# Attention products in one run per head pair, single-pass turns of copied softmax weights, and q stored as high, low, high

## The chip, the core and the metric

The kernel runs on one core of one Trainium2 chip. Five engines work side by side: TensorE (PE in the profile; its weight loads PEld), VectorE (DVE), ScalarE (ACT), GpSimd (POOL) and SyncE (SP), which issues every DMA here. The metric is the device time of one launch in microseconds (us); lower is better. Times shown are medians of several runs.

## What is computed

Attention with a top-k mask on 2 batches, 8 heads, 576 tokens and head size 64, then two dense blocks over all 1152 tokens of width 512:

```
scores = scale * q @ k.T                      # per batch and head, 576 x 576
kth    = the 32nd largest of each row
attn   = softmax(where(scores >= kth, scores, -1e9))
x      = (attn @ v), heads side by side       # 1152 x 512
p      = domain_probs / sum(domain_probs)     # 1152 x 4
x      = sum over 4 experts e of p[:, e] * (relu(x @ w1[e]) @ w2[e])   # 512 -> 1024 -> 512
out    = ((x @ w_a) * (x @ w_b)) @ w_out      # 512 -> 1536 -> 512, weights in double precision
```

## The kernel before

**Tiles and groups.** Tokens are taken in nine tiles of 128: four per batch, and a mixed one (MIX) with the last 64 tokens of both batches. `SIZES` puts them in groups of 1, 2, 3 and 3. A step is one tile and one pair of heads; there are 36, in the order group, head pair, tile. n is the number of the step: 0 to 3 belong to group 0, 4 to 11 to group 1, 12 to 23 to group 2, 24 to 35 to group 3, the last one of each pair being the mixed tile.

**One step.** `scores` multiplies q and k, both split into a high and a low part in fp32r. k's parts lie one above the other on the partitions (k high, k low), turned by TensorE. q is stored with four blocks of 64 per tile, high, high, low, low, and two turned operands come of them: (high, high) and (low, low). ACT moves the scores to SBUF. `masked` finds the 32 largest of each row on VectorE (four MAX8, three MATCH_REPLACE8 per head), then makes the masked exponentials: ACT, GpSimd, ACT, a sum, a reciprocal, and ACT's scaling in place (L773). At step `URGENT` = 3 `hurried` takes a shorter way over VectorE. `weigh` turns the scaled weights (`e`) on TensorE, four blocks of 128 columns and one of 64 per head (L821, L822), evicts them with two ACT instructions per head (L828, L832), and multiplies by v: for each tile one run of ten pairs of f32 matmuls (twenty for the mixed tile), the two heads of a pair side by side in the array's columns (L848). The last block of v (`vrem`) has 64 real rows and 64 of zeros. When a head pair of a group is done, ACT and VectorE split the sum into `xs` (L866, L868).

**The experts.** When all four head pairs of a group are there, its tokens go through the four experts: `plain` for group 0 in f32, `experts` for the others in fp32r with split operands (three matmuls for one). Weights come by DMA into four slots (`raw`), are split by ACT (L889) and GpSimd or VectorE (L890). `gated` at the end does the last block for all tokens.

**What sets the order.** All work is recorded as operations with a key, a cost and what they wait for; `Plan` simulates the engines with these costs and emits each engine's instructions in the order so found, the best of 42 tries. Instructions then execute in that fixed order on each engine. On TensorE keys put attention first, experts' matmuls (1000 and up) fill. The plan's price of a DMA is on L88: 500 ns to issue, 320 GB/s, 2100 ns to land; of a turn on L320; of a run with v on L854. `mm` (L458) and `tr` (L461) issue every matmul and every turn, so the profile knows them by those two lines, and by the names of what they read: a turn reads `identr`; turns of `low` are softmax weights (f32), of `big` q and k (fp32r), of `ys` the experts' sums. A run with v reads `low` with `128*64`; score matmuls read `big` with 288 columns.

**Memory.** SBUF is laid out in regions (`big`, `mid`, `raw`, `low`) with numbered slots; a region is used again by a later stage when the earlier slots are done. `krem`, the split last rows of k, has a fixed place at the start of `big`.

## Time and profile before

| | |
|---|---|
| time, median of 3 runs | 841.81 us (841.73 to 843.05) |
| span of the profiled execution | 838.8 us, from its first to its last instruction |
| TensorE busy | 816.7 us, 97% |
| VectorE busy | 702.5 us, 84% |
| ACT busy | 540.0 us, 64% |
| GpSimd busy | 265.7 us, 32% |
| DMA queue of SyncE | 116 MB, 43.9% of 16 engines' span |

The page gives no time of the profiled execution but its span; the median of the timed runs is 3.0 us longer, which stands for what lies around the span. Matmuls are pipelined: the duration of one in the profile is longer than its place in the stream, so costs on TensorE are read from start to start. An f32 matmul leaves two records, an fp32r matmul and any turn one.

### The profile page before, as it was taken

To read this page: it belongs to the slowest core of one execution; us is meant where nothing else is said; L and a number is where in the kernel's file an instruction comes from. 1 tells how busy PE (TensorE), PEld (TensorE's weight loads), DVE (VectorE), ACT (ScalarE), POOL (GpSimd) and SP (SyncE) were. 2 spreads that over 40 slices of the span, in tenths; PEclk is the share of its full clock that TensorE was granted. 3 is DMA by queue.
4 is the path that set the end of the run, shared out by engine and by line. 5 is a ranking of instruction groups with operands and counts; after the bars stand their busy time and mean duration, and the time that the engine had idled before them with its cause. 6 is when DMAs were issued, how large, how long until landed. Compare 5 with 4: busy or idle time off the path is not lost.

```text
span 838.8 us, 14118 instructions
## 1 busy us (share of the span) xinstructions
PE 816.7 (97%) x5177; PEld 730.4 (87%) x5177; DVE 702.5 (84%) x1363; ACT 540.0 (64%) x1037; POOL 265.7 (32%) x250
## 2 busy tenths in 40 slices
PE   7599999999999999999999999999999999999997
PEld 6477877789898999899989998999898989999996
DVE  7999999999999999999969998545235888899723
ACT  6888887989999989887666556343125535344220
POOL 3634443797998966763110000000000000000000
PEclk9999999999999999999999999999999999999999
DMA  5849977754555435233335656433002322323003
GB/s 176 286 120 313 308 240 236 218 175 165 192 172 178 148 138 182 84 95 101 101 126 169 208 158 220 126 125 101 1 1 63 89 78 73 101 78 100 26 1 113
DMA packets 83509, 117.06 MB, mean 140 GB/s; under 512 B 10608, under 2 KB 54640, under 8 KB 83440
## 3 DMA queue, kind: packets, MB, share of 16 engines
q1 hardware_dynamic: 83440, 116.17, 43.9%
q8 instruction: 40, 0.66, 0.3%
q14 instruction: 29, 0.24, 0.1%
HBM read 109.07 MB, written 7.08 MB: 138 GB/s over the span
## 4 chain that ended last, share of the span: by engine, by line
PE 80%; DVE 14%; ACT 4%; issue 1%; POOL 0%; DVEq 0%; POOLq 0%; ACTq 0%
PE ps L458 76%; DVE low L723 7%; DVE low L731 6%; PE ps L461 5%; ACT mid L889 1%; ACT low L773 1%; ACT low L762 1%; ACT low L703 0%; ACT low L828 0%; ACT low L754 0%; ACT big L514 0%; ACT big L655 0%; DVE low L794 0%; POOL low L758 0%; DVE low L1175 0%
## 5 line engine op out<-in xcount | busy, mean ns | idle before, releaser
L723 DVE MAX8 low<-low 128x8 f32<-128x576 f32 x288 | 203.3, 745 | 2.8 <-ACT low L703 2.6
L458 PE MATMUL ps<-xs,mid 128*128 128x384 f32 (+1 forms) x1152 | 204.6, 320 | 0.3 <-DVE mid L963 0.2
L458 PE MATMUL ps<-mid 128*128 128x512 f32 x768 | 196.8, 394 | 0.0
L458 PEld LDWEIGHTS ps<-xs,mid 128*128 128x128 f32 x1152 | 184.9, 188 | 9.1 <-DVE xs L1024 0.5
L458 PEld LDWEIGHTS ps<-mid 128*128 128x128 f32 x768 | 140.0, 188 | 22.6
L731 DVE MATCH_REPLACE8 low<-low 128x576 f32<-128x576 f32 x216 | 159.1, 741 | 0.0
L458 PE MATMUL ps<-xs,big 128*128 128x384 f32 x864 | 152.6, 335 | 0.0
L458 PEld LDWEIGHTS ps<-xs,big 128*128 128x128 f32 x864 | 150.2, 188 | 1.5 <-DVE xs L1024 0.3
L889 ACT ACTIVATE mid<-raw 128x1024 fp32r<-128x1024 f32 x96 | 101.7, 1062 | 44.4 <-PE ps L458 33.9
L890 POOL TENSOR_TENSOR mid<-raw,mid 128x1024 fp32r<-128x1024 f32 x48 | 115.2, 2407 | 13.8 <-ACT mid L889 9.5
L758 POOL TENSOR_TENSOR low<-low 128x576 f32<-128x576 f32 x70 | 99.6, 1438 | 31.9 <-ACT low L754 30.4
L890 DVE TENSOR_TENSOR mid<-raw,mid 128x1024 fp32r<-128x1024 f32 x48 | 59.3, 1236 | 24.6 <-ACT mid L889 24.1
L959 ACT ACTIVATE mid<-ps 128x384 fp32r<-128x384 f32 (+1 forms) x96 | 43.8, 457 | 52.5 <-PE ps L458 51.5
L458 PE MATMUL ps<-big,mid 128*128 128x512 f32 x324 | 76.1, 391 | 0.0
L458 PEld LDWEIGHTS ps<-big,mid 128*128 128x128 f32 x324 | 60.5, 188 | 12.6 <-DVE low L1175 0.6
L963 DVE SCALAR_TENSOR_TENSOR mid<-ps,mid 128x384 fp32r<-128x384 f32 (+1 forms) x96 | 48.3, 505 | 25.0 <-ACT mid L959 24.6
L1154 ACT ACTIVATE low<-ps 128x384 f32<-128x384 f32 x36 | 17.7, 492 | 69.7 <-PE ps L458 69.3
L773 ACT ACTIVATE low<-low 128x576 f32<-128x576 f32 x70 | 51.3, 774 | 12.1 <-DVE low L770 12.0
L762 ACT ACTIVATE low<-low 128x576 f32<-128x576 f32 x70 | 54.4, 778 | 2.2 <-POOL low L758 2.1
L461 PE MATMUL ps<-identr,low 128*128 128x128 f32 (+1 forms) x360 | 50.6, 283 | 4.7 <-ACT low L773 4.0
L754 ACT ACTIVATE low<-low 128x576 f32<-128x576 f32 x70 | 52.3, 776 | 4.3 <-POOL low L748 4.3
L703 ACT ACTIVATE low<-ps 128x576 f32<-128x576 f32 x72 | 46.6, 650 | 11.4 <-POOL low L758 7.5
(90 smaller groups left out, 1024.8 us busy)
## 6 DMA issues: line engine op xcount, KB each, us to landing
raw<-in_moe_w_dram SPq DMA_DIRECT2D x122, 512.0 KB, 3.8
big<-kscr SPq DMA_DIRECT2D x20, 576.0 KB, 5.5
low<-in_v_dram SPq DMA_DIRECT2D x24, 256.0 KB, 3.9
low<-in_moe_w_a_dram SPq DMA_DIRECT2D x12, 512.0 KB, 4.3
low<-in_moe_w_b_dram SPq DMA_DIRECT2D x12, 512.0 KB, 3.8
low<-in_moe_w_out_dram SPq DMA_DIRECT2D x12, 512.0 KB, 3.6
kscr<-big SPq DMA_DIRECT2D x8, 576.0 KB, 4.7
ys<-in_moe_w_dram SPq DMA_DIRECT2D x6, 512.0 KB, 5.2
```

Source lines behind the costliest of these rows:

```text
L458: nc.tensor.matmul(out, l, r, **kw)
L461: nc.tensor.transpose(out, a, i)
L703: S, lambda: nc.scalar.activation(s.ap.rearrange("p (c n) -> p c n", c=2), at.ap[:, :, 0:HALF], AF.Copy),
L723: 62 + 1.04 * width, lambda at=at, cs=cs: nc.vector.max(m8v()[:, x, cs], at()), key + 0.02 * r, [done],
L731: lambda at=at, cs=cs: nc.vector.match_replace(out=src[1](), in_to_replace=m8v()[:, x, cs], in_values=at(), imm_value=LOW),
L754: S, lambda x=x, s=s: nc.scalar.activation(e[x].ap, s.ap, AF.Relu, bias=endv()[:, x, 1:2], scale=-STEEP),
L758: pool_(S), lambda x=x, s=s: nc.gpsimd.tensor_tensor(e[x].ap, s.ap, e[x].ap, op=ALU.subtract), ks, [a], [s, e[x]]
L762: lambda x=x: nc.scalar.activation(e[x].ap, e[x].ap, AF.Exp, bias=endv()[:, x, 0:1], scale=scale, accum_out=sums.ap[:, x:x + 1]),
L773: S, lambda x=x: nc.scalar.activation(e[x].ap, e[x].ap, AF.Copy, scale=sums.ap[:, x:x + 1]),
L889: hi = scalar(1024, lambda: nc.scalar.activation(u.ap[:, 0:1024], r.ap, AF.Copy), 500 + s, [ld], [u, r], sbuf=True)
L890: sub = lambda eng: eng.tensor_tensor(u.ap[:, 1024:2048], r.ap, u.ap[:, 0:1024], op=ALU.subtract)
L963: lambda h=h, p=p: nc.vector.scalar_tensor_tensor(h.ap[:, n:2 * n], p.ap[:, 0:n], 0.0, h.ap[:, 0:n], op0=ALU.max, op1=ALU.subtract),
```

## The change

- `weigh` keeps the turned weights of all tiles of a group and head pair, and multiplies them by v in one run at the last tile. A tile's weights for both heads lie in one buffer of 2 x 576 columns. Nine blocks of 128 are turned in place of ten: the fifth holds the last 64 columns of head 0 and the first 64 of head 1. k of the odd head has its last rows first, and `vrem` has its zeros in the other half for odd heads. Evictions are one per head, 512 and 640 columns wide.
- From step 8 (`MOVED`) each head's scaled weights are copied by a DMA from `e` to a buffer `er` of type fp32r, and the turns read that one.
- q is stored as high, low, high; the two turned operands are the overlapping views (high, low) and (low, high). The subtraction that makes the low part writes 64 columns per tile and head in place of 128.
- `krem` becomes slots of `big`, where `er` follows it. `e` has three slots of two heads in place of six of one, `pt` four of 1152 in place of three of 640. The scratch area for DMAs issued by GpSimd is set to 1024 bytes per partition.
- The plan's price of a run with v is 1092 ns a tile and 350 ns a run (1245 a tile before); of fp32r turns 46 + 85 for each of all but two + 64.

```diff
+AV, SWITCH = 1092, 350
+MOVED = 8
-    krem = [big.t[0:REM, b * 1024:(b + 1) * 1024].rearrange("p (h a d) -> p h a d", a=2, d=D) for b in range(B)]
-    big.at = 2048
+    krems = big.slots("krem", B, 1024)
...
+    ers = big.slots("er", 2, 2 * S)
+    ers.rank = 0.5
-    es = low.slots("e", 6, S)
-    pts = low.slots("pt", 3, (M4 + 1) * 128)
+    es = low.slots("e", 3, 2 * S)
+    pts = low.slots("pt", 4, 2 * S)
...
+    def split2(dst, src, m, key, after, tiles, eng):
+        a = scalar(
+            m * 2 * D, lambda: nc.scalar.activation(dst()[:, :, ::2], src().unsqueeze(2).to_broadcast([128, m, 2, D]), AF.Copy),
+            key, after, tiles, sbuf=True,
+        )
+        sub = lambda e: e.tensor_tensor(dst()[:, :, 1], src(), dst()[:, :, 0], op=ALU.subtract)
...
-                        tr(p[:, i, lh], sqv()[:, j, i, lh].rearrange("p a d -> p (a d)"), identr)
+                        tr(p[:, i, lh], sqv()[:, j, i, lh:lh + 2].rearrange("p a d -> p (a d)"), identr)
...
 def weigh(pair, i, ed, n):
+        (e, done), p, ptd = ed, pts.tile(n), []
+        f, idt = e, ident
+        if n >= MOVED:
+            f, idt = ers.tile(n), identr
+            done = [load(
+                lambda j=j: f.ap[:, j * S:(j + 1) * S].bitcast(F32), lambda j=j: e.ap[:, j * S:(j + 1) * S], n + 0.1, [done[j]], [e, f], S * 512,
+            ) for j in range(2)]
...
+        for j in range(2):
+            at = atts.tile(kt)
+            def turn(j=j, at=at):
+                a = (at.ap if f is e else at.ap.bitcast(F32R)).rearrange("p b n -> p (b n)")
+                if j:
+                    tr(a[:, MAIN - 128:MAIN], f.ap[:, MAIN:MAIN + 128], idt)
                 for m in range(M4):
-                    tr(a[:, m], e.ap[:, m * 128:(m + 1) * 128], ident)
-                tr(a[0:REM, M4], e.ap[:, MAIN:S], ident)
+                    c0 = j * (S + REM) + m * 128
+                    tr(a[:, j * MAIN + m * 128:j * MAIN + (m + 1) * 128], f.ap[:, c0:c0 + 128], idt)
-            o = tensor(4 * TURN_F + 80, turn, kt, [done, ready], [at, e])
+            hold = (M4 + j) * TURN_F if f is e else 46 + (M4 + j - 2) * 85 + 64
+            o = tensor(hold, turn, kt, [done[j], done[0], ready], [at, f])
...
+        pair.turned.append((t, p, ptd))
+        if i < T - 1:
+            return
         def emit():
+            for i, (t, p, _) in enumerate(pair.turned):
+                for r0, r1, b in [(0, 128, t[0])] if t != MIX else [(b * REM, (b + 1) * REM, b) for b in range(B)]:
                     for m in range(M4 + 1):
                         for j in range(2):
...
-        pair.od.append(tensor(
-            1245, emit, n + 0.6, ...
+        pair.od = [tensor(
+            T * AV + SWITCH, emit, n + 0.6, ...
```

On TensorE, the second tile of group 2's first head pair, before: its ten turns (`identr,low`, in two lots of four and one), and its run with v (`low`, `64x128`, and `vrem`), among score matmuls (`big`, `128x288`) and experts' matmuls of group 1 (`xs,mid` and `mid`):

```order
L461 MATMUL ps<-identr,low 128x128 x4
L461 MATMUL ps<-identr,low 64x128
L458 MATMUL ps<-xs,mid 128x256 x3
L461 MATMUL ps<-identr,low 128x128 x4
L461 MATMUL ps<-identr,low 64x128
L458 MATMUL ps<-mid 128x512 x9
L458 MATMUL ps<-low 64x128 x8
L458 MATMUL ps<-low,vrem_73 64x128 x2
L458 MATMUL ps<-big 128x288 x8
L458 MATMUL ps<-mid 128x512 x12
```

The first and the third tile of that pair have such a run of their own. In the changed program the same engine at the end of that pair:

```order
L464 MATMUL ps<-identr,big 128x128 x4
L461 MATMUL ps<-xs,mid 128x256 x18
L464 MATMUL ps<-identr,big 128x128 x5
L461 MATMUL ps<-big 128x288 x4
L461 MATMUL ps<-xs,mid 128x256 x6
L461 MATMUL ps<-low 64x128 x8
L461 MATMUL ps<-low,vrem_72 64x128 x2
L461 MATMUL ps<-low 64x128 x8
L461 MATMUL ps<-low,vrem_73 64x128 x2
L461 MATMUL ps<-low 64x128 x8
L461 MATMUL ps<-low,vrem_73 64x128 x2
L461 MATMUL ps<-big 128x288 x4
```

The three tiles' products stand in one run, and the turns, four and five, read `big`. In the whole program runs with v go from 36 to 16, f32 turns of softmax weights from 360 to 72, and 252 fp32r turns are new.

On TensorE, the end of group 1 in the changed program: group 0's experts (`raw,low`, `xf,ys`) run out, the last tile's nine turns, one more of those matmuls, the first three of group 1's experts, and the product of two tiles:

```order
L461 MATMUL ps<-xf,ys 128x128 x8
L461 MATMUL ps<-raw,low 128x512 x3
L464 MATMUL ps<-identr,big 128x128 x9
L461 MATMUL ps<-raw,low 128x512
L461 MATMUL ps<-xs,mid 128x256 x3
L461 MATMUL ps<-big 128x288 x4
L461 MATMUL ps<-low 64x128 x8
L461 MATMUL ps<-low,vrem_72 64x128 x2
L461 MATMUL ps<-low 64x128 x8
L461 MATMUL ps<-low,vrem_72 64x128 x2
```

Before, four matmuls of `raw,low` stood behind the last product of group 1, and none of group 1's experts ahead of it.

On SyncE's queue, the changed program in group 2: copies of softmax weights (`big<-low`) stand among loads of experts' weights (`raw<-in_moe_w_dram`), of v and of stored k (`big<-kscr`):

```order
L443 DMA raw<-in_moe_w_dram 128x4x256 x2
L443 DMA low<-in_v_dram 128x2x256
L443 DMA big<-kscr 128x1152
L443 DMA raw<-in_moe_w_dram 128x2x512
L443 DMA big<-low 128x576 x2
L443 DMA low<-in_q_dram 128x2x64
L443 DMA low<-in_q_dram 128x2x128
L443 DMA big<-low 128x576
L443 DMA raw<-in_moe_w_dram 128x2x512
L443 DMA big<-low 128x576
L443 DMA big<-kscr 128x1152
L443 DMA raw<-in_moe_w_dram 128x4x256 x2
```

The `big<-low` rows, 56 in the whole program, are new; a load behind one is issued after it.

## Rows read from the trace of the kernel before

**Rows 1.** The page's first line: span and instructions.

```profile
span 838.8 us, 14118 instructions
```

**Rows 2.** Stretches: us, busy of PE, PEld, DVE, ACT, POOL, clock, DMA, GB/s.

```profile
0.00:75.00 75.00, 58.41 (x390) 47.87 (x391) 69.76 (x156) 57.88 (x125) 33.58 (x54) 0.98 0.70 216
75.00:153.00 78.00, 77.90 (x582) 60.58 (x581) 78.00 (x169) 67.16 (x138) 33.06 (x39) 1.00 0.79 257
153.00:165.00 12.00, 11.62 (x96) 10.26 (x95) 12.00 (x27) 12.00 (x24) 10.78 (x9) 1.00 0.79 246
165.00:435.00 270.00, 269.58 (x2007) 243.09 (x2006) 261.91 (x541) 235.77 (x471) 188.25 (x151) 1.00 0.45 142
435.00:834.00 399.00, 398.99 (x2112) 368.64 (x2110) 279.86 (x472) 167.16 (x283) 0.00 (x0) 1.00 0.31 97
```

**Rows 3.** Chain that ended last: start, us, what (two pieces).

```profile
141.10 1.33 DVE low L723 x2
...
164.80 17.92 PE ps L458 x118
```

**Rows 4.** Timeline, TensorE, end of group 1: start, us, line, what.

```profile
142.12 1.28 PE L461 MATMUL ps<-identr,low 128*128 128x128 f32 x10
143.23 1.06 PE L458 MATMUL ps<-xf,ys 128*128 128x128 f32 x8
...
145.73 1.09 PE L458 MATMUL ps<-low 128*64 128x128 f32 x16
...
153.14 1.64 PE L458 MATMUL ps<-xs,mid 128*128 128x256 f32 x9
```

**Rows 5.** Timeline, TensorE, a mixed tile's run and q's turns.

```profile
323.73 0.69 PE L458 MATMUL ps<-low 128*64 128x64 f32 x16
324.25 0.29 PE L458 MATMUL ps<-low,vrem 128*64 128x64 f32 x4
324.36 0.64 PE L458 MATMUL ps<-low 128*64 128x64 f32 x16
324.83 0.29 PE L458 MATMUL ps<-low,vrem 128*64 128x64 f32 x4
...
326.22 0.64 PE L461 MATMUL ps<-identr,big 128*128 128x128 f32 x6
326.69 1.81 PE L458 MATMUL ps<-xs,mid 128*128 128x384 f32 x9
328.34 0.62 PE L461 MATMUL ps<-identr,big 128*128 128x128 f32 x6
```

**Rows 6.** Timeline, TensorE, 36 matmuls of 384 columns and what follows.

```profile
441.75 6.41 PE L458 MATMUL ps<-xs,mid 128*128 128x384 f32 x36
447.99 0.86 PE L458 MATMUL ps<-mid 128*128 128x512 f32 x3
```

**Rows 7.** Timeline, TensorE, one tile's run with v and its neighbours.

```profile
204.81 0.70 PE L458 MATMUL ps<-big 128*128 128x288 f32 x4
205.35 0.51 PE L458 MATMUL ps<-xs,mid 128*128 128x256 f32 x3
205.79 1.10 PE L458 MATMUL ps<-low 128*64 128x128 f32 x16
206.71 0.39 PE L458 MATMUL ps<-low,vrem 128*64 128x128 f32 x4
...
207.66 1.59 PE L458 MATMUL ps<-xs,mid 128*128 128x256 f32 x12
```

**Rows 8.** DMA issues: names, queue, count, KB each, median us to landing.

```profile
low<-in_v_dram SPq DMA_DIRECT2D x24, 256.0 KB, 3.9
...
kscr<-big SPq DMA_DIRECT2D x8, 576.0 KB, 4.7
...
out_dram<-low SPq DMA_DIRECT2D x8, 256.0 KB, 2.0
```

**Rows 9.** Waits of SyncE's queue: line, releaser, us in total, times, longest.

```profile
SPq L440 <- DVE mid L890: 150.6, 40, 9.1
```

More of the change, by code (lines that the diff above doesn't have):

```diff
@@ L396, in body @@
     wraws = raw.slots("wraw", 4, 1024)
[L397 removed]
+    low = Region("low", 12300 + 4 * 1152 - 3 * 640, F32)
     kraws = low.slots("kraw", 2, 2 * M4 * D)
@@ L519, in split @@
         return [a, b]
+    def split2(dst, src, m, key, after, tiles, eng):
[4 more added lines that the diff above has]
+        sub = lambda e: e.tensor_tensor(dst()[:, :, 1], src(), dst()[:, :, 0], op=ALU.subtract)
+        if eng == "DVE":
+            b = vector(dve(m * D) + 30, lambda: sub(nc.vector), key, [a], tiles, port=True)
+        else:
+            b = gpsimd(pool_(m * D), lambda: sub(nc.gpsimd), key, [a], tiles)
+        return [a, b]
     krem_done, vrem_done, qrem_done, kept = {}, {}, [], {}
+    krem = [krems.tile(b) for b in range(B)]
+    kremv = lambda b: krem[b].ap[0:REM].rearrange("p (h a d) -> p h a d", a=2, d=D)
     def keys(b, h2, key, eng):
@@ L670, in start_pair @@
             if b not in vrem_done:
-                vrem_done[b] = load(lambda b=b: vrem[b][0:REM], lambda b=b: last_rows(v, b), n - 2.4, (), (), 131072, since=14e3)
+                vrem_done[b] = [
+                    load(lambda b=b, j=j: vrem[b][j * REM:(j + 1) * REM, j::2], lambda b=b, j=j: last_rows(v, b)[:, j::2], n - 2.4, (), (), 65536, since=14e3)
+                    for j in range(2)
+                ]
         return pair
@@ L713, in masked @@
         urgent = n == URGENT
-        e = [es.tile(n) for _ in range(2)]
+        ep = es.tile(n)
+        ev = lambda x: ep.ap[:, x * S:(x + 1) * S]
         last, firsts = [], []
@@ L740, in masked @@
             key = n + (0.4 if urgent else 0.001) * x
-            last.append(top(x, [lambda s=s: s.ap, lambda x=x: e[x].ap], 0, TOPK // 8, S, key, sd[x][1]))
+            last.append(top(x, [lambda s=s: s.ap, lambda x=x: ev(x)], 0, TOPK // 8, S, key, sd[x][1]))
         if urgent:
@@ L838, in weigh @@
-        groups = [(0, 128, t[0])] if t != MIX else [(b * REM, (b + 1) * REM, b) for b in range(B)]
-        bs = [b for _, _, b in groups]
-        def emit():
-            for r0, r1, b in groups:
-                for m in range(M4 + 1):
-                    for j in range(2):
-                        vt = pair.v[b].ap.rearrange("p (h m d) -> p h m d", h=2, m=M4)
-                        l = vt[:, j, m] if m < M4 else vrem[b][:, pair.h + j]
-                        mm(
-                            ov()[j * D:(j + 1) * D, i, r0:r1], l, pt[j].ap[:, m * 128 + r0:m * 128 + r1],
-                            start=(m == 0), stop=(m == M4),
-                        )
@@ L853, in weigh @@
-        pair.od.append(tensor(
-            1245, emit, n + 0.6, [zeroed] + ptd + sum((pair.vd[b] for b in bs), []) + [vrem_done[b] for b in bs], [pair.o] + pt + [pair.v[b] for b in bs]
-        ))
+        (e, done), p, ptd = ed, pts.tile(n), []
[5 more added lines that the diff above has]
+            ) for j in range(2)]
@@ new lines, in weigh @@
+        pair.turned.append((t, p, ptd))
+        if i < T - 1:
+            return
+        def emit():
+            for i, (t, p, _) in enumerate(pair.turned):
+                for r0, r1, b in [(0, 128, t[0])] if t != MIX else [(b * REM, (b + 1) * REM, b) for b in range(B)]:
+                    vt = pair.v[b].ap.rearrange("p (h m d) -> p h m d", h=2, m=M4)
+                    for m in range(M4 + 1):
+                        for j in range(2):
+                            l = vt[:, j, m] if m < M4 else vrem[b][:, pair.h + j]
+                            c0 = j * (S + REM) + m * 128 if m < M4 else MAIN
+                            mm(ov()[j * D:(j + 1) * D, i, r0:r1], l, p.ap[:, c0 + r0:c0 + r1], start=(m == 0), stop=(m == M4))
@@ L856, in weigh @@
+        bs = batches(pair.tiles)
+        pair.od = [tensor(
+            T * AV + SWITCH, emit, n + 0.6, [zeroed] + sum((d for _, _, d in pair.turned), []) + sum((pair.vd[b] + vrem_done[b] for b in bs), []),
+            [pair.o] + [p for _, p, _ in pair.turned] + [pair.v[b] for b in bs],
+        )]
         if i == T - 1:
```

102 lines of the change are left out of this document (46 added, 56 removed).

## The prediction

> **What bounds the kernel now.** I read the stretches first, then the chain of work, then single runs of TensorE. The profiled execution spans 838.8 us [rows 1]; the median of the timed runs is 841.8, so 3.0 us lie around the span, and I carry them unchanged. In the stretches [rows 2] the reader is to see TensorE fill up: 58.4 us of the first 75, then 77.90 of 78, 11.62 of 12, 269.58 of 270 and 398.99 of 399, always at a granted clock of 1.00. Busy alone proves little where matmuls are pipelined, but the idle time does: 0.42 us in the 270. The chain [rows 3] says the same in another way: until 141.1 it is made of VectorE's top-k pieces (MAX8, MATCH_REPLACE8), then of a few ACT pieces, and from 164.8 on of TensorE runs. So there are two regimes. Up to about 153 us VectorE and TensorE are both full (78.00 and 77.90 of 78): VectorE with the top-k of groups 0 and 1, TensorE with group 0's experts as filling. From 153 on TensorE alone sets the time, and an instruction taken from it there is worth what it held. VectorE isn't far behind: 261.9 of 270 us between 165 and 435.
>
> **The change part by part.** *Turns.* A tile's softmax weights were ten f32 turns; such a run starts at 142.12, and the next kind of matmul at 143.23 [rows 4]: 1.11 us, 0.111 each. Now it is nine. For the eight tiles before step 8 that is 8 x 0.11 = 0.9 us, all before 153. For the other 28 the nine are fp32r turns. The trace has those for q: a run of six starts at 326.22, nine 384-column matmuls at 326.69, and the next run at 328.34 [rows 5]. A 384-column matmul takes 0.173 us ((447.99 - 441.75) / 36, [rows 6]), so the six took 2.12 - 1.56 = 0.56 us, 0.093 each, entry and exit included. Nine are 0.84; a tile saves 1.11 - 0.84 = 0.27 us. The 24 tiles of groups 2 and 3 lie behind 153: 24 x 0.27 = 6.5 us. The four of group 1 give 1.1 before it.
>
> By the Trainium skill, "TensorE: Matmul & The Clock Gate", section "LDWEIGHTS (loading the stationary operand)", a 128-column load takes columns / 1.2, 107 ns, and no kind of data is excepted. The f32 turn agrees with that, the fp32r turn at 93 ns doesn't; what the rule would leave of the change is a rival below.
>
> *Runs with v.* Before, each of the 36 tiles has its own run. One of them: four score matmuls at 204.81, three 256-column ones at 205.35, the run at 205.79, four score matmuls, and the next kind at 207.66 [rows 7]. From 205.35 to 207.66 are 2.31 us; less four score matmuls at 0.135 ((205.35 - 204.81) / 4) and three of 0.115 (two thirds of 0.173) this leaves 1.42 for the run. How much of it is entering and leaving? Its first sixteen records (an f32 matmul leaves two, and the two heads run as a pair, so eight pairs) take 0.92; the mixed tile shows two such groups in one run, 0.52 for the first and 0.47 for the second [rows 5], so 0.05 of the 0.92 is entry. 0.87 / 8 = 0.109 a pair, ten pairs 1.09: 0.33 us of a run are the switch. The order has 16 runs in place of 36. Groups 2 and 3 lose 16 switches behind 153, 5.3 us; group 1 loses 4 before it, 1.3.
>
> *The sum on TensorE*: 6.5 + 5.3 = 11.8 us behind 153, 0.9 + 1.1 + 1.3 = 3.3 before it.
>
> *What of the 3.3 counts.* There VectorE's pace stays as it is; TensorE can gain only as far as group 1's last product doesn't wait for it. Step 11's turns are at 142.12, its product at 145.73, group 1's experts start at 153.14 [rows 4]. In the new order only one matmul of filling is left between the last turns and that product, and the path to it gets a copy and both tiles' products. Bounds: nothing, and all of 3.3; I take the middle, 1.6, since neither end has a nearer row.
>
> *The copies* are the wait that the change adds. From step 8 each head's weights (288 KB, 56 copies) go through SyncE's queue from one place of SBUF to another before TensorE turns them. No row shows such a copy. 256 KB land in 2.0 us towards HBM and in 3.9 from it, 576 KB in 4.7 [rows 8]; the plan counts (line 88) 500 ns, 294,912 bytes at 320 GB/s and 2100 ns, 3.5 us. So a copy can be 1.5 us earlier or 1.2 us later than planned. TensorE executes in a fixed order: behind a late turn wait the experts' matmuls. If each of 24 tiles waits 1.2, that is 28.8 us; if TensorE, once it has slipped by 1.2, stays behind ACT and VectorE, which don't wait for it, it is 1.2 once. I take 1.5, near the second end: waits for ACT's scaling, planned in the same way, left only 0.42 us idle in 270 [rows 2]. By the Trainium skill, "SBUF — State Buffer", section "The DMA setup-cost knee", a transfer takes 2 us plus its bytes at 436 GB/s: an estimate of 2.7 us here, no wait, and a forecast of 828.4. The rows have 3.9 for 256 KB, where it gives 2.6, so I don't go by it.
>
> Behind a copy on SyncE's queue stand weight loads. SyncE spends 150.6 us waiting until VectorE frees a slot, up to 9.1 at once [rows 9]: loads go out when a slot of four falls free, so some microseconds more are hidden by the three others. If this cover went, each tile would cost TensorE what the copy waited: the rival on the slow side.
>
> *At nothing:* half the evictions of turned weights (72 for 144, one of each pair wider) and half-size subtractions for q, because ACT (235.8 of 270) and GpSimd (188.3) don't hold up a TensorE that is idle for 0.42; the zeroing, the smaller scratch area and the tiles' new places, because no instruction on the path waits for them. q's turns stay as many.
>
> *Sum:* 11.8 + 1.6 - 1.5 = 11.9 us; a span of 838.8 - 11.9 = 826.9, and with the 3.0 around it **829.9 us**.
>
> **The rivals.** *Late copies or late attention, partly.* The turns wait 0.3 us in each of the 24 tiles, 7.2 us, or the attention ends late: in the new order only 24 matmuls of 384 and 36 of 512 columns of group 2's experts stand behind the last product (before: 96 and 84), 24 x 0.173 + 36 x 0.23 (four thirds of it) = 12.4 us of cover. For it: VectorE's 261.9 of 270. Against it: if VectorE can't go faster at all, it is late by the 11.8 that TensorE gains, still inside the 12.4. The time: 841.8 - 13.4 + 7.2 = 835.6.
>
> *The turns gain only the tenth.* Were an fp32r turn bound as an f32 one, a tile would save 0.11: 24 x 0.11 = 2.6 in place of 6.5, 0.4 in place of 1.1 before: 834.2. Against it: 0.093 for 0.111 in the trace. By the Trainium skill, "TensorE: Matmul & The Clock Gate", section "LDWEIGHTS (loading the stationary operand)", it would be so.
>
> *SyncE's order makes it slower.* A copy at the head of the queue waits for ACT, and with it the loads behind. From 11.8 / 24 = 0.5 us of TensorE's waiting per tile the gain is gone; at 0.8, two thirds of the 1.2 above, it is 841.8 - 13.4 + 19.2 = 847.6. For it: all loads share this one queue and SyncE already waits most of the time. Against: four slots of lead.
>
> *The change doesn't do what it says*: excluded for the number of runs and the kinds of turn, which the order shows; whether a turn of copied data is as quick as one of q's is in the second rival.
>
> **How the numbers follow.** The forecast 0.68, alone with a range of 825.5 (15.1 saved, and 1.2 more if each switch is 0.06 dearer than read) to 834 (copies that cost 4 in place of 1.5, and nothing of the 3.3); partly late 0.17; tenth turn alone 0.05; slower 0.10. Within 0.2% (1.7 us) a measurement of this kernel can't tell a change. Faster by more: 0.68 + 0.05 + 0.13 of the partly late = 0.86; same: 0.04 of that and 0.01 of the slow one; slower 0.09. The range that leaves out the slow rival and a few hundredths on each side is 825.5 to 839.
>
> **What would show it.** Runs with v: 16, each costing TensorE about 0.33 + T x 1.09 us. fp32r turns of four and five: about 0.37 and 0.47 us from start to start of what follows, less that work's own time. TensorE's idle time between 165 and the end of the attention: under 2 us, with DMA as its releaser where the copies are late. The first experts' matmul of group 1 between 150 and 154 us. The last run with v at about 440 us, and no gap at the start of group 3's experts. Copies landing in 2.0 to 4.7 us. I am wrong if the runs cost more than counted (a run of 20 or 30 matmuls slower per pair than 0.109), if the idle time in 165 to 435 grows beyond 5 us, or if the start of group 1's experts moves past 156.

## The result and the profile after

The changed kernel took 846.93 us (median of 4 runs, 845.69 to 848.14) against 841.77 before: a ratio of 1.0067, 95% interval 1.0055 to 1.0079. 829.9 us were forecast, with 839 as the upper end. The profiled span is 843.9 us, 5.1 more than [rows 1].

First the stretches of the changed kernel, as in [rows 2], and two short ones behind them (us; busy time of PE, PEld, DVE, ACT, POOL; clock; DMA share; GB/s):

```profile
0.00:75.00 75.00, 55.41 (x365) 45.27 (x366) 68.10 (x152) 56.95 (x115) 30.90 (x53) 0.89 0.66 204
75.00:153.00 78.00, 73.84 (x569) 58.00 (x569) 77.48 (x168) 63.32 (x115) 32.39 (x38) 1.00 0.92 301
153.00:165.00 12.00, 11.53 (x90) 10.14 (x85) 12.00 (x29) 11.61 (x25) 7.75 (x10) 1.00 0.66 233
165.00:435.00 270.00, 260.93 (x1954) 237.59 (x1954) 257.86 (x531) 230.30 (x420) 182.29 (x147) 0.98 0.58 188
435.00:834.00 399.00, 398.99 (x2152) 369.19 (x2151) 285.78 (x483) 174.05 (x293) 3.24 (x4) 1.00 0.32 99
275.00:300.00 25.00, 18.00 (x102) 15.66 (x100) 23.27 (x49) 21.17 (x40) 16.07 (x16) 0.90 0.51 177
300.00:325.00 25.00, 24.11 (x173) 21.91 (x173) 23.43 (x51) 21.56 (x44) 11.99 (x15) 0.89 0.40 129
```

The same two short stretches of the kernel before:

```profile
275.00:300.00 25.00, 25.00 (x197) 22.94 (x197) 24.95 (x55) 23.78 (x53) 20.50 (x17) 1.00 0.58 194
300.00:325.00 25.00, 25.00 (x203) 22.34 (x199) 24.78 (x54) 22.71 (x47) 17.32 (x15) 1.00 0.29 96
```

TensorE, never idle there before, is idle for 7 of 25 us, and its clock falls. I added up every idle gap between TensorE's instructions in both traces. Before: 17.5 us in all, 17.1 of them ahead of 165. After: 33.3 us, of which 19.6 ahead of 75 (16.6 before), 4.6 in 75 to 165 (0.5 before) and 9.1 between 165 and the last run with v of group 2 (0.4 before). The rest of the span, "not idle" below, fell from 821.3 to 810.6 us. So 10.7 us less of work and 15.8 more of idling make the 5.1.

What TensorE does in 288 to 306 of the changed kernel (timeline: start, us, line, what, and in brackets the idle time ahead with its releaser):

```profile
288.10 0.66 PE L464 MATMUL ps<-identr,ys 128*128 128x128 f32 x4 [1.50 <-DVE xs L1051]
290.74 0.80 PE L461 MATMUL ps<-xs,mid 128*128 128x384 f32 x3 [1.99 <-DVE xs L1051]
...
294.38 1.57 PE L461 MATMUL ps<-big 128*128 128x288 f32 x8
299.34 0.72 PE L464 MATMUL ps<-identr,big 128*128 128x128 f32 x4 [3.39 <-DMA big<-low]
300.96 0.85 PE L464 MATMUL ps<-identr,big 128*128 128x128 f32 x5 [0.89 <-DMA big<-low]
...
303.86 1.83 PE L461 MATMUL ps<-low 128*64 128x128 f32 x16
```

And the same place before, 14 us earlier:

```profile
289.67 1.09 PE L458 MATMUL ps<-low 128*64 128x128 f32 x16
...
292.55 0.93 PE L458 MATMUL ps<-mid 128*128 128x512 f32 x3
293.32 0.62 PE L461 MATMUL ps<-identr,big 128*128 128x128 f32 x6
293.78 2.49 PE L458 MATMUL ps<-xs,mid 128*128 128x384 f32 x13
```

The run at 303.86 is that of step 23, the last of group 2, whose experts can't be finished without it. I call its start the product. Before, it stood at 289.67, and group 1's experts, the filling, lasted until 293.1: the two met almost exactly, and group 2's experts followed without a gap. After, the filling is used up at 282.2 (eleven microseconds earlier: TensorE has less to do, and the new order puts more of the filling ahead of the attention) and the run comes at 303.86, fourteen later. Between the two TensorE has the tip of group 2's experts, the turns and the scores, and waits. The clock pays too:

```profile
290.00:295.00 5.00, 4.26 (x21) 4.13 (x22) 5.00 (x14) 2.89 (x6) 2.23 (x4) 0.67 0.55 206
295.00:300.00 5.00, 1.61 (x11) 1.28 (x9) 4.56 (x9) 3.84 (x6) 1.41 (x2) 0.84 0.31 118
300.00:305.00 5.00, 4.11 (x26) 3.77 (x27) 5.00 (x13) 3.78 (x8) 1.78 (x3) 0.50 0.02 5
```

At 300 to 305, behind the idle 3.39 us, the granted clock is 0.50: 1.2 in place of 2.4 GHz. Busy time times the share of clock that is missing, from 290 to 305, is 3.7 us (0.33 x 4.26 + 0.16 x 1.61 + 0.50 x 4.11). I had counted 15.1 us less of work (11.8 + 3.3); 10.7 were seen. These 3.7 are of the size of the difference, but the sum isn't closed: the first 75 us ran at a lower clock too, 0.89 in place of 0.98 [rows 2].

The waits of TensorE in the changed kernel (us in total, times, longest), the four largest:

```profile
PE ps L464 <- ACT low L793: 8.3, 3, 4.2
PE ps L464 <- DMA big<-low: 7.2, 6, 3.4
PE ps L464 <- ACT low L722: 3.8, 3, 2.9
PE ps L464 <- POOL big L520: 2.7, 1, 2.7
```

L793 is ACT's scaling of the softmax weights, L722 its move of the scores to SBUF, L520 GpSimd's subtraction in the splits. These three lie ahead of 75 us, but for 0.4 of L722's; of the waits on copies 2.4 us lie between 75 and 165 and 4.8 behind 165.

Copies and the loads of weights (rows as in [rows 8]):

```profile
raw<-in_moe_w_dram SPq DMA_DIRECT2D x122, 512.0 KB, 4.4
big<-low SPq DMA_DIRECT2D x56, 288.0 KB, 3.7
```

The copies landed in 2.3 to 6.4 us. What TensorE executes was sized right. Two copied heads' turns and a run with v over three tiles:

```profile
227.49 0.46 PE L464 MATMUL ps<-identr,big 128*128 128x128 f32 x4
227.78 0.59 PE L461 MATMUL ps<-xs,mid 128*128 128x256 f32 x3
...
228.91 0.54 PE L464 MATMUL ps<-identr,big 128*128 128x128 f32 x5
229.28 0.77 PE L461 MATMUL ps<-big 128*128 128x288 f32 x4
229.88 0.87 PE L461 MATMUL ps<-xs,mid 128*128 128x256 f32 x6
230.69 1.09 PE L461 MATMUL ps<-low 128*64 128x128 f32 x16
...
231.83 1.04 PE L461 MATMUL ps<-low 128*64 128x128 f32 x16
...
232.92 1.04 PE L461 MATMUL ps<-low 128*64 128x128 f32 x16
...
234.11 0.81 PE L461 MATMUL ps<-big 128*128 128x288 f32 x4
```

Four turns and five take 0.29 and 0.37 us from start to start, 0.073 each, where q's six took 0.47 in the same reading [rows 5], 0.078 each. A tile inside a run costs 1.09 us (232.92 - 231.83), as forecast, and the whole run 3.54 (234.11 - 229.88, less six 256-column matmuls at 0.115), where 0.33 + 3 x 1.09 = 3.60 were forecast.

### The profile page after: what moved, and what is told of

Same layout as the page of the kernel before. It is cut to its first block, busy times and chain, and to the rows that moved or that the text cites. A ratio compares the mean times of both kernels' runs of the same rounds, so it can differ in the third digit from the quotient of the medians.

```text
span 843.9 us, 14148 instructions
## 1 busy us (share of the span) xinstructions
PE 806.0 (96%) x5141; PEld 724.2 (86%) x5141; DVE 704.7 (83%) x1363; ACT 536.2 (64%) x965; POOL 256.6 (30%) x249
## 4 chain that ended last, share of the span: by engine, by line
PE 86%; ACT 4%; DMA 4%; DVE 3%; POOL 1%; issue 1%; SPq 0%; POOLq 0%; ACTq 0%; DVEq 0%
PE ps L461 81%; PE ps L464 6%; DMA big<-low 3%; DVE low L743 1%; DVE low L751 1%; ACT low L793 1%; ACT low L722 1%; DMA raw<-in_moe_w_dram 1%; POOL mid L917 1%; ACT big L671 0%; ACT low L774 0%; POOL big L520 0%; SPq L443 0%; DVE xs L1051 0%; ACT low L859 0%
## 5 line engine op out<-in xcount | busy, mean ns | idle before, releaser
L461 PE MATMUL ps<-xs,mid 128*128 128x384 f32 (+1 forms) x1152 | 207.2, 322 | 2.7 <-DVE xs L1051 2.0
L461 PE MATMUL ps<-mid 128*128 128x512 f32 x768 | 194.3, 393 | 0.1
L461 PEld LDWEIGHTS ps<-xs,mid 128*128 128x128 f32 x1152 | 184.2, 189 | 10.9 <-DVE xs L1051 2.5
L464 PEld LDWEIGHTS ps<-identr,big 128*128 128x128 f32 (+1 forms) x476 | 53.0, 146 | 27.7 <-ACT low L722 5.2
L464 PE MATMUL ps<-identr,big 128*128 128x128 f32 (+1 forms) x476 | 61.4, 260 | 15.3 <-DMA big<-low 7.2
L986 ACT ACTIVATE mid<-ps 128x384 fp32r<-128x384 f32 (+1 forms) x96 | 44.3, 463 | 38.2 <-PE ps L461 37.7
L990 DVE SCALAR_TENSOR_TENSOR mid<-ps,mid 128x384 fp32r<-128x384 f32 (+1 forms) x96 | 48.2, 505 | 22.8 <-ACT mid L986 22.2
L793 ACT ACTIVATE low<-low 128x576 f32<-128x576 f32 x70 | 51.9, 785 | 7.1 <-DVE low L790 7.0
## 6 DMA issues: line engine op xcount, KB each, us to landing
big<-low SPq DMA_DIRECT2D x56, 288.0 KB, 3.7
```

The costliest lines, as they stand in the source:

```text
L461: nc.tensor.matmul(out, l, r, **kw)
L464: nc.tensor.transpose(out, a, i)
L793: S, lambda x=x: nc.scalar.activation(ev(x), ev(x), AF.Copy, scale=sums.ap[:, x:x + 1]),
L986: n, lambda h=h, p=p: nc.scalar.activation(h.ap[:, 0:n], p.ap[:, 0:n], AF.Relu), -1000, [o], [h, p]
L990: lambda h=h, p=p: nc.vector.scalar_tensor_tensor(h.ap[:, n:2 * n], p.ap[:, 0:n], 0.0, h.ap[:, 0:n], op0=ALU.max, op1=ALU.subtract),
```

## The experiments

Five theories are tested. A: before group 2's last product TensorE doesn't set the time, so what it saves there turns into idling, and the copies' latency adds to it. B: the order that the planner drew was unlucky (it draws lateness at random and keeps its best order). C: the start is late by 1.9 us. D: a turn that waits for its copy holds PSUM slots which the scores of three steps later need, and so holds up VectorE. E: the time that TensorE saves goes to the filling too early, which takes ACT, VectorE and GpSimd from the attention.

All runs are in one table. "Step 23" is the end of that step's last MAX8 (the 192nd of the trace), "product" the start of group 2's last run with v, "filling" the start of the last matmul of group 1's experts, "idle" TensorE's before 165 and from there to 5 us past that run; "not idle" the span less all idling. The time is a median, and each ratio is to the kernel before as measured beside that kernel (medians of 840.72 to 841.37; 841.77 for the changed one). The columns behind the ratio come from one profiled execution, which lies up to 1.7 us from the median (843.66 for 845.35 in per_tile_runs). Where an expectation counts matmuls of the filling ahead of a step's scores, it counts the steps from one: its step 24 is n = 23.

| kernel | us | ratio to before, 95% | step 23 | product | filling | idle | not idle |
|---|---|---|---|---|---|---|---|
| before | 841.77 | | 271.6 | 289.7 | 293.1 | 17.1, 0.4 | 821.3 |
| before_other_draws | 842.83 | 1.0008-1.0026 | 272.7 | 289.3 | 297.1 | 16.7, 0.6 | 824.0 |
| before_third | 842.23 | 1.0002-1.0019 | 271.5 | 287.6 | 297.6 | 18.4, 1.0 | 822.0 |
| q_split_only | 841.79 | 0.9998-1.0017 | 271.3 | 284.9 | 296.4 | 19.1, 0.0 | 821.7 |
| fill_early | 841.34 | 0.9996-1.0013 | 277.4 | 292.6 | 289.1 | 18.0, 0.4 | 820.7 |
| after | 846.93 | 1.0055-1.0079 | 284.0 | 303.9 | 282.2 | 24.2, 9.1 | 810.6 |
| other_draws | 842.04 | 0.9992-1.0013 | 278.9 | 299.7 | 284.2 | 20.7, 7.2 | 812.6 |
| after_third | 847.99 | 1.0052-1.0081 | 284.2 | 305.3 | 292.1 | 22.9, 9.0 | 814.2 |
| per_tile_runs | 845.35 | 1.0032-1.0066 | 276.6 | 299.8 | 293.0 | 23.8, 3.2 | 814.2 |
| no_copies | 841.70 | 0.9997-1.0016 | 278.3 | 295.4 | 288.0 | 23.9, 1.7 | 813.8 |
| direct | 844.06 | 1.0022-1.0045 | 276.0 | 292.9 | 302.4 | 22.0, 8.8 | 810.8 |
| copies_late | 839.76 | 0.9971-0.9990 | 275.9 | 295.9 | 289.1 | 22.8, 1.9 | 813.2 |
| scores_first | 839.30 | 0.9964-0.9983 | 274.0 | 297.7 | 283.0 | 23.5, 3.4 | 810.3 |
| scores_first_draws | 839.82 | 0.9974-0.9997 | 276.2 | 299.3 | 287.6 | 22.3, 4.2 | 811.0 |
| group3_only | 837.47 | 0.9948-0.9973 | 269.7 | 295.0 | 289.7 | 19.8, 0.9 | 814.1 |
| group3_scores_first | 838.73 | 0.9959-0.9982 | 271.6 | 298.0 | 295.6 | 20.5, 1.2 | 815.5 |
| late_scores_first | 835.52 | 0.9921-0.9948 | 269.5 | 293.4 | 289.5 | 23.7, 0.7 | 809.1 |
| late_draws | 848.62 | 1.0075-1.0103 | 287.7 | 306.6 | 282.4 | 22.2, 8.6 | 816.3 |
| late_paced | 838.75 | 0.9957-0.9982 | 270.6 | 289.8 | 300.5 | 23.9, 3.4 | 810.4 |
| paced | 848.68 | 1.0079-1.0107 | 279.9 | 299.5 | 305.1 | 23.3, 10.9 | 810.9 |

**no_copies.** All weights by f32 turns, no copy.

```diff
-MOVED = 8
+MOVED = 99
```

> The changed kernel with MOVED = 99: no step copies its weights, all 36 tiles have nine f32 turns; one run with v per group and head pair, and q's new split, stay. Theory A (the copies lie in a path that VectorE and the end of group 2 pace: they bring the last product of group 2 from 299.8 to 303.9 us while group 1's experts run out 11 us earlier): without them TensorE's idle time between 250 and 325 us falls from 8.7 us to under 1.5, and the time is 841.8 less what is saved behind group 2's end (8 switches of 0.33 and 12 tiles of 0.11, 4.0 us): 836 to 840. Theory B (the order found by the plan's draws is a matter of luck): no closer forecast than 836 to 850. Theory C (what acts before step 8 delays the start: step 3's last MAX8 ended at 49.6 for 47.9, and granted clock 0.72 between 25 and 50): the start stays late, step 3 ends after 49, and the time is 843 or more.

841.7 us, idle in 275 to 300 about 1 us:

```profile
275.00:300.00 25.00, 23.96 (x195) 21.75 (x194) 24.97 (x55) 23.27 (x46) 18.36 (x18) 1.00 0.46 148
```

It is 5 us faster than the changed kernel, in one draw of each (the changed kernel's three draws are 6 us apart). A's 836 to 840 was missed: without any copy the product still comes at 295.4, 5.7 us later than before, and the nine turns and 20 switches fewer bring nothing over before.

**direct.** ACT's scaling writes fp32r into the tile that is turned; fp32r turns, no copies.

```diff
+        fp = ers.tile(n) if n >= MOVED else ep
-                S, lambda x=x: nc.scalar.activation(ev(x), ev(x), AF.Copy, scale=sums.ap[:, x:x + 1]),
+                S, lambda x=x: nc.scalar.activation(fp.ap[:, x * S:(x + 1) * S], ev(x), AF.Copy, scale=sums.ap[:, x:x + 1]),
```

> The changed kernel without copies: from step 8 ACT writes the scaled weights straight into the fp32r buffer that TensorE turns (rounded to fp32r, which the copies don't do), everything else as in the changed kernel, fp32r turns too. Theory A: the time is 841.8 less 8 switches of 0.33 and 12 tiles of 0.29 behind group 2's end, 6.1 us: 833 to 838, and TensorE idle under 1.5 us between 250 and 325. If it is not the copies' delay but the turns or the longer runs with v that hurt, it stays at 844 or more. Theory C: 841 or more.

844.1 us: A's 833 to 838 was missed. TensorE waits for the filling's own weights, ACT's rounding and GpSimd's subtraction:

```profile
249.99 0.50 PE L461 MATMUL ps<-mid 128*128 128x512 f32 x1 [2.06 <-ACT mid L914]
252.44 1.22 PE L461 MATMUL ps<-mid 128*128 128x512 f32 x2 [1.96 <-POOL mid L915]
```

With no copy at all the gain was still lost, to other waits: 8.8 us of idling behind 165.

**copies_late.** Copies and fp32r turns in group 3 alone.

```diff
-MOVED = 8
+MOVED = 24
```

> The changed kernel with MOVED = 24: only group 3's twelve tiles are copied and turned in fp32r. Theory A: groups 1 and 2 end as without copies, and group 3's end has some 12 us of group 2's experts as cover: 834 to 838. If copies hurt wherever they are (SyncE's order, waits for weight loads): 841 or more, with TensorE idle between 325 and 470 us, where the changed kernel has none. Theory C: 841 or more.

839.8: 0.1 to 0.3% faster than before, between the two expectations, and 1.8 us beyond A's.

**other_draws.** The changed kernel, other random numbers.

```diff
-            draw = random.Random(r)
+            draw = random.Random(r + 1000)
```

> The changed kernel, only with other random draws in the plan's 42 tries. Theory A: the idle time at group 2's end is a matter of the path, not of the draw: 844 to 849. Theory B: the time moves by more than 3 us from 846.9, or the idle time between 250 and 325 us falls under 3 us.

842.0: A's 844 to 849 was missed. Of B's two signs the first came (4.9 us from 846.9), the second didn't: the idle time behind 165 is still 7.2 us.

**q_split_only.** The kernel before with the new `split2` for q and the two overlapping views.

```diff
-                        tr(p[:, i, lh], sqv()[:, j, i, lh].rearrange("p a d -> p (a d)"), identr)
+                        tr(p[:, i, lh], sqv()[:, j, i, lh:lh + 2].rearrange("p a d -> p (a d)"), identr)
```

> The kernel before with nothing changed but q's split (high, low, high; half-size subtractions; the two overlapping views turned). TensorE has the same turns, so theory A (what TensorE saves before 300 us turns into idle time, and the copies make it worse) expects 840 to 843 us. Theory C (the late start) expects, if the late start of 1.9 us comes from q's split, step 3's last MAX8 at 49.5 us or later in place of 47.9 and about 843; if that MAX8 stays at 47.9, the late start comes from the softmax weights' side (wider evictions, paired slots) and not from q.

841.8, no difference, as expected. Step 3's last MAX8 is at 48.8, between C's two cases. C falls by before_other_draws and before_third below: the kernel before ends step 11 there at 134.3 and 133.9, as late as the changed kernel (133.9; 132.0 before), and loses no more than 1.5 us.

**per_tile_runs.** The changed kernel with a run with v per tile.

```diff
-        if i < T - 1:
-            return
+        def emit(i=i, t=t, p=p):
```

> The changed kernel with one run with v per tile again (36 in place of 16), all else as changed. By my sum TensorE gets back 20 switches of 0.33 us, 6.6 us, of which 5.3 behind 153 us. If TensorE's work alone set the time: 846.9 + 5.3 = 852. Theory A: the work of groups 1 and 2 fills idle time there, only group 3's 8 switches (2.6 us) count: 847 to 850. Rival (the merged runs themselves hold up the end of a group, since nothing of a pair is done until its last tile): the last product of group 2 earlier by 2 us or more than 303.9 and a time of 843 to 846.

845.4, within the rival's range; A's 847 to 850 was missed. TensorE has 20 switches more to do and the time is no longer: 1.6 us less than the changed kernel's, within the spread of the two (843.7 to 846.3 and 845.7 to 848.1). The product comes 4.1 us earlier, and the 8 switches of group 3 (2.6 us) stand behind it. Where TensorE alone sets the time, 5.3 us more would have shown.

**before_other_draws.** The kernel before:

```diff
-            draw = random.Random(r)
+            draw = random.Random(r + 1000)
```

> The kernel before with the planner's random draws taken from other seeds (r + 1000), which moves instructions and changes none. Theory B (the change's loss is in good part luck of the draw, which moved the changed kernel by 5 us): 844 us or more, or 838 or less. Theory A (the loss comes from what was changed, and before is no lucky draw): 840 to 843.

842.8: 1.5 us over before, within A's range. Before, the draw hardly matters.

**scores_first.**

```diff
-        kt = n + (-0.45 if n == URGENT else 0.5)
+        kt = n + (-0.45 if n == URGENT else 0.7 if n >= MOVED else 0.5)
```

> The changed kernel with the turns' need in PSUM set behind that of the scores of three steps later (step + 0.7 in place of step + 0.5, from step 8 on), so that a turn which waits for its copy doesn't hold the two slots that those scores need. Theory D (a late copy reaches VectorE by this queue for PSUM): the last MAX8 of step 18 comes by 4 us earlier against step 17's than in the changed kernel, TensorE's idle time at 275 to 300 falls below 3 us from 7.0, and the time is 840 to 844. Theory A (the latency itself at the end of group 2): last product of group 2 still at 302 us or later and 845 to 848.

839.3, under D's range; idle in 275 to 300 is 2.3 us, and step 18 ends 12.1 us behind step 17 in place of 18.2. The product comes at 297.7, against A's 302 or later. What D meant, in the changed kernel (PE first, then DVE): step 15's turns come at 207.30 and 208.36, only then the scores of step 18, and VectorE gets its next MAX8 at 210.22.

```profile
207.30 0.46 PE L464 MATMUL ps<-identr,big 128*128 128x128 f32 x4
...
208.36 0.55 PE L464 MATMUL ps<-identr,big 128*128 128x128 f32 x5
208.74 0.76 PE L461 MATMUL ps<-big 128*128 128x288 f32 x4
```

```profile
203.71 0.75 DVE L743 MAX8 low<-low 128x8 f32<-128x576 f32 x1
...
207.92 0.42 DVE L990 SCALAR_TENSOR_TENSOR mid<-ps,mid 128x256 fp32r<-128x256 f32 x1 [1.74 <-ACT mid L986]
210.22 0.76 DVE L743 MAX8 low<-low 128x8 f32<-128x576 f32 x1 [1.88 <-ACT low L722]
```

**scores_first_draws**, the same with other draws:

```diff
-            draw = random.Random(r)
+            draw = random.Random(r + 1000)
```

> The changed kernel with the turns' need in PSUM behind that of the scores (step + 0.7) and the planner's draws from other seeds (r + 1000). Theory D (the queue for PSUM makes a late copy hold up VectorE, and the change of need cures it whatever the draw): 837 to 841, and under other_draws (842.0) by 1.5 us or more. Theory B (the 839.3 was a lucky draw): 842 or more.

839.8, 2.2 us under other_draws, as D expected. D's edit gained in both draws of the changed kernel.

**group3_only.** copies_late with a run per tile before step 24, so that only group 3 is changed.

```diff
-        if i < T - 1:
+        if n >= MOVED and i < T - 1:
             return
+        first = 0 if n >= MOVED else i
```

> The changed kernel with everything that touches the softmax weights' path taken back before step 24: f32 turns and no copies there, one run with v per tile there. In group 3 (steps 24 to 35) it is as changed: twelve copied tiles with fp32r turns (12 x 0.27 = 3.2 us) and 4 runs with v in place of 12 (8 x 0.33 = 2.6 us). Theory A (only what TensorE saves behind group 2's last product counts, since before it the attention, not TensorE, sets the time): 841.4 - 5.8 + 1.9 for the late start = 837.5, within 836 to 839, and no later than copies_late (839.8). If savings before group 2's end counted too, this kernel would lose 8 switches more than copies_late: 842 or more.

837.5, on A's number. It has twelve switches more than copies_late (four in group 1 and eight in group 2; the expectation forgot the four), all ahead of group 2's last product, and is no slower: 0.2% faster by the ratios, whose intervals just overlap, with the product 0.9 earlier. It was run in one draw, and draws move such kernels by more than this; the same pair with D's edit, below, comes out the other way.

**late_scores_first.** copies_late with the need of scores_first from step 8 on.

```diff
-        kt = n + (-0.45 if n == URGENT else 0.5)
+        kt = n + (-0.45 if n == URGENT else 0.7 if n >= 8 else 0.5)
```

> copies_late (copies and fp32r turns only in group 3) with the turns' need in PSUM at step + 0.7 from step 8 on. Theory D with A: no copy is left before group 2's end, so the change of need has little to cure: 838 to 840.5, within 1 us of copies_late (839.8). If the order of need gains by itself, without copies: 837 or less.

835.5, the fastest, 0.52 to 0.79% under before. It lies below the range of D with A, and where the order of need would gain by itself; the next run speaks against that. Its two stretches:

```profile
275.00:300.00 25.00, 25.00 (x211) 23.16 (x210) 25.00 (x55) 23.82 (x46) 24.22 (x16) 1.00 0.67 227
300.00:325.00 25.00, 25.00 (x146) 22.96 (x145) 25.00 (x55) 22.87 (x45) 15.26 (x16) 1.00 0.58 196
```

Step 23 ends at 269.5 and no gap is left.

**group3_scores_first**, the same edit in group3_only:

```diff
-        kt = n + (-0.45 if n == URGENT else 0.5)
+        kt = n + (-0.45 if n == URGENT else 0.7 if n >= 8 else 0.5)
```

> group3_only with the turns' need in PSUM at step + 0.7 from step 8 on. Theory A: 836 to 839, within 1 us of group3_only. If the order of need gains by itself: 2 us under group3_only.

838.7, 1.3 us slower than group3_only: the need in PSUM is no sure gain by itself. This kernel has the same twelve switches more than late_scores_first, ahead of the product, and is 3.2 us slower than it. Twelve switches at 0.33 are 4.0 us. TensorE is hardly idle behind 165 in either (1.2 and 0.7 us), and there the savings ahead of the product did count.

**late_draws.** The fastest kernel's rules, other draws.

```diff
-            draw = random.Random(r)
+            draw = random.Random(r + 1000)
```

> late_scores_first (835.5, the fastest so far) with the planner's draws from other seeds (r + 1000): the same rules, but an order with 522 matmuls of the filling before the scores of step 24 in place of 366. Theory E: step 23's last MAX8 at 275 or later in place of 269.5, TensorE idle 2 us or more in 275 to 310, and 839 to 843. Theory D (the order of need for PSUM does it, whatever the draw): 834 to 838.

848.6, beyond E's 839 to 843, though step 23 ends late (287.7) and TensorE idles as E said; it is against D. The same rules in two draws are 13 us apart:

```profile
275.00:300.00 25.00, 20.85 (x168) 18.81 (x167) 24.75 (x52) 22.03 (x45) 16.39 (x18) 0.93 0.37 116
300.00:325.00 25.00, 21.36 (x153) 19.18 (x152) 23.42 (x52) 21.94 (x45) 11.91 (x14) 0.86 0.39 128
```

**fill_early.** The kernel before, group 1's weights urgent on ACT.

```diff
-        hi = scalar(1024, ..., 500 + s, [ld], [u, r], sbuf=True)
+        hi = scalar(1024, ..., -100 if s < 200 else 500 + s, [ld], [u, r], sbuf=True)
```

> The kernel before with the high parts of group 1's weights made urgent on ACT, which pulls the filling ahead a little: 411 matmuls before the scores of step 23 (384 before), 291 before those of step 21 (255), 513 before those of step 25 (468). TensorE saves nothing and there are no copies. Theory E: step 23's last MAX8 2 to 4 us later than 271.6, some TensorE idle time (1 us or more) between 275 and 315, and 843 to 846. If the filling only goes along and the change's own parts do the harm: 840 to 842.

841.3, where E expected 843 to 846. Half of E holds: with filling taken earlier the attention ends late (step 23 by 5.8 us), but the time is the same, and TensorE isn't idle:

```profile
275.00:300.00 25.00, 25.00 (x192) 22.92 (x190) 24.42 (x54) 24.02 (x52) 19.81 (x17) 1.00 0.56 177
```

**paced.** The changed kernel with the filling's weights held back.

```diff
+        since = 140000 + 4500 * paced[0]
+        paced[0] += 1
-        ld = load(..., 500 + s, (), [r], 512 << 10)
+        ld = load(..., 500 + s, (), [r], 512 << 10, since=since if paced[0] <= 32 else 0.0)
```

> The changed kernel with one thing added: the loads of group 1's 32 weight units are held back in the plan (unit k not before 140 + 4.5 k us), so that 414 matmuls of the filling stand before the scores of step 24, as in the kernel before (420; in the changed kernel 537). Copies, fp32r turns, runs with v, the order of need for PSUM: all as changed. Theory E (filling too early): step 23's last MAX8 at 272 to 277 us in place of 284.0, TensorE idle under 2 us in 275 to 300, the time 837 to 842. Theory D (the queue for PSUM) and theory A (copies' latency) change nothing here: 844 or more.

848.7: E missed. Step 23 comes 4.1 us earlier, but TensorE waits 8.24 us at one place for a copy that took 6.6 us, with no filling to stand in:

```profile
202.32 0.52 PE L461 MATMUL ps<-xs,mid 128*128 128x256 f32 x3
211.08 0.72 PE L464 MATMUL ps<-identr,big 128*128 128x128 f32 x4 [8.24 <-DMA big<-low]
```

**late_paced**, the same in the fastest kernel:

```diff
+        since = 140000 + 4500 * paced[0]
+        paced[0] += 1
```

> late_scores_first with group 1's weight loads held back as in paced: 360 matmuls of the filling before the scores of step 24 (366 without). Theory E: nothing is left to gain from the filling there, 834 to 837.5; step 23's last MAX8 within 268 to 272. If holding loads back gains by itself (a freer SyncE queue): 833 or less.

838.8, 3.2 us slower than without, outside E's 834 to 837.5: holding the filling back is no remedy.

**after_third and before_third**, a third draw of each:

```diff
-            draw = random.Random(r)
+            draw = random.Random(r + 2000)
```

> The changed kernel with a third set of the planner's draws (r + 2000). In the order, 474 matmuls of the filling stand before the scores of step 24 (537 in the changed kernel, 489 in other_draws). If the change itself takes the gain back by TensorE's idle time, whatever the draw: 840 to 846, TensorE idle 25 us or more in all and about 811 us not idle. If the result on record was an unlucky draw and no more: 836 or less.

> The kernel before with the same third set of draws: 414 matmuls of the filling before the scores of step 24 (420 before). Its TensorE has no work to run out of, so the order matters little: 839.5 to 843.5, TensorE idle 17 to 20 us, about 821 us not idle. A time outside this would mean that the order alone moves this kernel too as much as it does the changed one.

848.0 and 842.2; the first lies beyond the 840 to 846 that was expected, the second within its range. Draw by draw the changed kernel stands at 846.9, 842.0 and 848.0 against 841.8, 842.8 and 842.2: slower by 5 to 6 us in two draws, level in one, and idle for 28 to 33 us in each. Before spreads by 1 us, the changed one by 6.

## Why the prediction was wrong

**The step that failed** is the sentence "From 153 on TensorE alone sets the time, and an instruction taken from it there is worth what it held." It was read from 0.42 us of idling in 270 [rows 2]. But that stretch was full because the filling happened to last as long as the attention of group 2: to 293.1 and 290.9. Two limits met there, and TensorE's busy share can't tell one from two. That VectorE was busy for 24.95 of 25 us in 275 to 300 hinted at the other. In the changed kernel the two come apart by 22 us (filling to 282.2, product at 303.9), and TensorE waits: 8.7 us more idling behind 165, and 3.7 of missing clock. Together, 12.4 us, they take back the 11.8 that the sum counted there. Ahead of 165 idling grew by 7.1 us, against 3.3 counted; 2.4 of the 7.1 are waits on copies, and the rest wasn't taken apart.

**How far the table bears this out.** In the ten kernels that have all of group 3's savings and whose filling ends before the product, the time less the product is 540.5 to 543.9 us, while the product moves from 293.4 to 306.6: behind the product each has about the same work left on TensorE. no_copies and per_tile_runs, which lack the fp32r turns or the longer runs of group 3, lie above all ten, at 546.3 and 545.6. In the five kernels at the top of the table, where the filling lasts about as long as the attention and TensorE idles for at most 1.0 us behind 165, the time stays within 841.3 to 842.8 while the product moves from 284.9 to 292.6. The table doesn't show that every saving ahead of the product is lost. Where TensorE has no gap it can still count: late_scores_first and group3_scores_first differ by twelve switches there, and by 3.2 us. The sentence fails for the changed kernel in all three draws, by the idle time; it isn't wrong for every order.

**The terms on TensorE** were right: turns, tiles in a run, and the runs' number. The start of group 1's experts moved from 153.14 to 149.67, more than the 1.6 I had taken of the 3.3; three of its matmuls now stand ahead of group 1's last product, and the time didn't follow.

**The copies** were mis-sized: 1.5 us against 7.2, the sum of TensorE's waits on them. I priced their landing (2.0 to 4.7 us; it was 2.3 to 6.4) and took it that TensorE, once behind, stays behind. Behind 282 it had no filling to be behind with. What they cost the whole kernel isn't settled: no_copies is 5 us faster than the changed kernel, but scores_first keeps all 56 copies and is 7.6 faster.

**"At nothing"** for ACT and GpSimd rested on the same idle time, and direct showed 2 us waits for both.

**The rivals.** "Partly late" had the mechanism, late attention, at the wrong place: I checked the cover at group 3's end (12.4 us) and not at group 2's (about 3 us). The slow rival's 847.6 comes near the time, not by its mechanism: TensorE's waits on copies add up to 7.2 us, six in number, not 0.8 in each of 24 tiles, so that near hit is luck. "The turns gain only the tenth" fell with 0.073 us a turn. Of the things that would prove me wrong, one came: over 5 us idle in 165 to 435 (9.1). Of the signs, the last run with v came at 462.8 in place of 440. "Always at a granted clock of 1.00" overlooked the 0.98 of the first stretch; nothing hangs on it. Nor do 3.0 us lie around a span: the four runs of the changed kernel took 1.7 to 1.8 us more than their spans (845.69 for 843.9), so the profiled execution of before was some 1.2 us quicker than its median. The forecast was taken from the median and stays the same. The order showed beforehand that the filling would be used up sooner: 537 of its 576 matmuls stand ahead of the last scores of step 23, 420 before. It didn't show the time: paced has 414 there and took 848.7.

**Why the attention of group 2 is late**, by 6 to 13 us at step 23 against the same draw of the kernel before, is settled in part. These are the stretches from the end of step 11's top-k to that of step 23's, before and after (columns as in [rows 2]):

```profile
132.00:271.60 139.60, 138.80 (x1061) 121.08 (x1060) 137.86 (x298) 130.47 (x259) 116.08 (x90) 1.00 0.60 188
133.90:284.00 150.10, 146.47 (x1123) 129.28 (x1118) 142.69 (x306) 134.02 (x242) 123.81 (x93) 1.00 0.71 230
```

MAX8 and MATCH_REPLACE8 take as long in both, 119.1 and 119.5 us. Of the 10.5 us more, VectorE is idle for 5.7 (7.4 after, 1.7 before) and busy with other work, most of it filling, for some 4.5. In the other two draws it idles for 5.1 and 10.1 us, where the kernel before with the same draws has 1.2. Its longest waits after are D's, a MAX8 for scores that ACT (L722) moves late, and the filling's, for ACT's L986:

```profile
DVE low L743 <- ACT low L722: 2.9, 3, 1.9
DVE mid L990 <- ACT mid L986: 2.6, 3, 1.7
```

The first is 3.1 and 5.9 us in the other two draws, at most 1.1 in the three of before, and gone in scores_first and its second draw, where VectorE idles for 1.6 and 2.7 us. So D's order of need for PSUM is one cause that is shown. Copies aren't the whole of it: no_copies has 2.4 us of the same wait.

**Not settled.** What else holds the attention and the product back. Without copies step 23 still ends at 278.3, with D's edit at 274.0, and by the draw alone at 269.5 or 287.7; no one edit accounts for it. no_copies, direct, copies_late, group3_only and per_tile_runs were run in one draw each, so a difference of a few microseconds between them can be the draw's. The 3 us more idling before 75 come in gaps near 22, 32 and 52 us; what brings them about stays open.

## What to carry to other kernels

When an engine is full because independent filling is put into its gaps, ask at the end of each stage which ends first, the filling or the work that the next stage waits for; if they end together, time saved on that engine ahead of this point can turn into idling there, and only what lies behind it is sure to count. A planner's order is part of the measurement: try each version with two or three draws before a change of half a per cent is believed. A wait added to a chain that feeds the second limit can cost its latency even if the full engine seems to hide it, for what waits also holds buffers that the second limit needs.

## What the runs showed of the hardware

A 288 KB copy within SBUF landed in 2.3 us at best. In the changed kernel it took up to 6.4 us, when a 576 KB load and a load of weights had been issued within 2 us ahead of it, and in per_tile_runs up to 8.2 us, behind two loads of weights. The 512 KB weight loads took 4.4 us in the median beside 56 copies, 3.8 before and 3.7 in no_copies. fp32r turns run at 0.073 us each, start to start, against 0.111 for f32 [rows 4]. TensorE's granted clock was 0.67 at 290 to 295, where TensorE had just idled for 1.50 and 1.99 us, and 0.50 at 300 to 305, behind 3.39 us of idling; it was 1.00 again at 310 to 315, where TensorE was busy throughout.
